# Eight input loads of the first batch asked for by GpSimd's queue instead of SyncE's, in an RWKV and Fourier-mixing kernel on one core

## The chip, the core and the metric

The kernel runs on one core of a Trainium2 chip. The metric is device time in microseconds (us). Before the change the median of three runs is 185.66 us (185.46 to 186.11). One execution was taken by the hardware profiler: it took 186.69 us, of which 184.6 us are the span that the profile shows. Times below that name a place ("at 8.86") are us from the start of that span.

## What is computed

Inputs r, k, v, w have the shape 4 batches x 8 heads x 768 steps x 48, in float32. The first half is a recurrent attention:

```python
for t in range(S):
    cur = einsum('bhd,bhe->bhde', u * k[t], v[t])
    y[t] = einsum('bhd,bhde->bhe', r[t], state + cur)
    state = w[t][..., None] * state + einsum('bhd,bhe->bhde', k[t], v[t])
```

The result, seen as 768 rows of 384 per batch, goes through a mixing block: the real part of a Fourier transform over both axes is added to it, each row is brought to mean 0 and variance 1, and a two-layer network follows (384 to 1536, relu, 1536 to 384), whose result is added to the rows:

```python
u = x + real(fft(fft(x, axis=1), axis=2))
un = (u - mean(u)) / sqrt(var(u) + 1e-6)
out = u + relu(un @ w_ch1) @ w_ch2
```

## The kernel before

**Tiling.** Each batch is cut into 6 chunks of 128 steps; `attention(b, c)` does one. It needs four loads, one each of w, k, r and v, of 128 x 384 float32 (192 KB). In HBM a head's step is a run of 48 floats, so one load moves 1024 pieces of 192 bytes. Here a load is called by tensor, batch and chunk: r(0,1) is r of batch 0, chunk 1. Seven buffers per tensor hold loads that are ahead of the work.

What a chunk does, in lines of the profile: ScalarE takes the logarithm of w (tile `lb`, L533) and casts v to bf16 (`vb`, L533); TensorE adds the logarithms up by triangular matrices (L724, L728, L734, L737); ScalarE takes exponentials (L730, L743, tile `e`); VectorE and GpSimd form the products `rk` (r times k, then times u, L519), `dc` (their sum over a head, L751), `vtd` (v times that sum, L519) and the scaled `rkh` (L519 for k, L762 for r); TensorE transposes these (L778, L784; evictions `rkt`, L542 or L543) and makes the scores (L794), VectorE masks them (L799, `ah`), TensorE multiplies by v and by the state (L820, L841, L844), and VectorE adds `vtd` (L850).

`mix(b)` then does the Fourier sums (L908, L931), the statistics (L933 to L939), the normalised rows `un` (L524 or L533), their transposes (L954, evicted to `unt`) and the two layers (L978 with the first weight matrix, called W1, and L996 with the second, W2). W1 and W2 are asked for once, by GpSimd's queue (L702), and become bf16 on their way; `W_AFTER` makes W1's ask wait for w(0,3) and W2's for r(1,0).

**Order.** Nothing is scheduled at run time. Every piece of work is recorded as an operation, and the table `ORDER` says, engine by engine, in which order the operations stand; "sp" is SyncE's list, which holds the loads (`load_one`, L563), the stores and a few transposes by DMA, and "pool" is GpSimd's. Each engine runs its list strictly in order, and an operation waits by semaphores for those it depends on. `_Prog.schedule` replays the list with fixed costs; the only things taken from its times are the PSUM bank of each tile and the order in which an instruction's waits are written. 32 matmuls that compute nothing (L1053, "warm") stand in TensorE's list to fill gaps, and 26 more stand at its beginning (L1017).

In the opening SyncE asks for r(0,0), k(0,1), w(0,1), u, k(0,0), v(0,0), w(0,0), w(0,2), r(0,1), k(0,2), r(0,2), r(0,3), w(0,4) and so on; GpSimd's list begins with ten fills and index patterns, and its next work is the scaled k of chunk 2 (L519, `rkh`).

Of the kernel before, what the change touches and what calls it, by code (L numbers as in the profile page):

```python
# [7 lines left out]
ALU = mybir.AluOpType  # L8
# [19 lines left out]

W_AFTER = {"W1": (0, 3, "w"), "W2": (1, 0, "r")}

NW = 32
# [4 lines left out]
        "6 74 1438 1439 1440 1441 1442 101 100 127 103 153 129 155 70 113 126 1443 1444 165 112 119 139 138 116 "  # L36
        "66 142 1445 1446 1447 1448 205 179 181 178 152 121 207 1449 1450 68 1451 1452 1453 1454 145 164 147 190 "
        "191 171 1455 168 1456 1457 231 217 194 255 204 1458 173 1459 1460 242 230 216 197 1461 1462 1463 1464 "
        "1465 220 1466 241 263 256 1467 427 199 426 257 1468 245 429 225 264 223 455 265 485 456 1469 248 458 "
        "258 266 259 487 271 272 273 274 275 468 260 276 267 277 278 268 279 280 281 282 303 294 439 438 445 304 "  # L40
        "285 305 286 287 467 295 296 323 332 314 333 324 315 474 325 471 334 310 292 301 316 497 359 343 345 349 "
        "347 355 442 353 351 339 484 365 361 330 477 321 363 357 382 367 368 372 496 448 373 500 369 513 503 514 "
        "516 386 374 506 547 525 388 526 548 384 398 529 390 532 550 377 580 535 581 559 378 560 396 591 379 566 "
        "592 563 394 406 777 779 595 776 568 404 400 392 402 598 806 808 407 613 789 788 411 805 412 408 621 622 "
        "792 614 615 623 616 624 617 625 618 605 626 606 627 607 608 609 610 628 629 630 631 632 864 835 837 866 "
        "653 795 635 636 654 655 644 645 646 637 416 818 817 413 417 673 824 821 664 665 666 660 418 651 674 642 "
        "675 853 834 847 798 705 715 703 707 701 699 898 827 693 900 846 863 711 682 697 695 876 683 713 850 684 "
        "717 722 882 897 931 910 718 709 856 875 909 671 723 879 913 719 680 727 885 724 1117 930 1119 728 689 "
        "729 916 750 918 942 941 742 1116 732 1143 1145 752 746 736 1132 945 734 1169 748 1142 1171 744 738 955 "
        "948 754 740 971 766 972 1129 767 973 1158 1168 956 768 957 958 974 963 975 959 960 1155 976 977 978 979 "  # L50
        "980 981 982 964 965 966 967 968 1135 985 1184 999 1000 1001 986 987 1195 1023 1197 1194 1009 992 1226 "
        "1256 993 1024 1025 994 761 762 763 1016 1181 1228 1161 1017 1018 1010 1011 1225 756 757 1210 1207 758 "
        "1187 1255 1055 1045 1039 1035 1051 1033 1037 1049 1041 1047 1043 1213 1057 1067 1238 1062 1058 1053 "
        "1068 1243 1082 1080 1059 1076 1084 1241 1267 1063 1069 1072 1092 1285 1270 1277 1286 1088 1287 1278 "
        "1064 1279 1074 1293 1294 1295 1094 1296 1297 1280 1281 1298 1282 1299 1300 1288 1301 1302 1303 1304 "
        "1289 1290 1086 1307 1321 1308 1314 1331 1309 1322 1323 1090 1078 1315 1345 1316 1338 1339 1096 1332 "
        "1101 1346 1333 1347 1340 1106 1102 1097 1107 1098 1103 1108 1365 1355 1357 1361 1367 1369 1377 1371 "
        "1363 1359 1394 1414 1373 1402 1406 1398 1412 1416 1379 1404 1375 1384 1400 1396 1380 1389 1408 1381 "
        "1390 1423 1385 1391 1386 1410 1428 1424 1418 1419 1425 1420 1429 1430 1433 1434 1435"),
    "act": (  # L60
        "0 20 21 22 23 24 25 26 109 99 125 151 102 104 156 130 128 71 115 61 140 141 177 203 167 67 182 154 180 "
        "161 135 208 166 69 229 193 233 219 206 187 238 244 232 218 62 454 425 213 243 483 430 459 252 428 457 "
        "435 261 269 283 284 441 270 488 447 440 469 309 291 311 293 344 346 338 360 348 499 356 350 340 354 312 "
        "366 322 486 358 383 313 493 364 512 341 476 515 517 546 387 505 549 527 528 385 522 389 579 551 391 582 "
        "556 561 583 399 534 562 397 593 775 594 395 780 342 588 778 862 804 393 401 403 541 809 405 790 807 574 "
        "791 604 785 833 619 611 633 838 814 843 620 867 797 634 820 819 659 650 641 662 826 652 643 849 836 716 "
        "706 896 708 702 872 663 704 700 1115 901 865 906 696 698 714 855 929 878 933 899 670 712 710 911 691 "
        "672 679 688 692 681 938 1125 884 932 690 1167 1141 891 1120 751 944 943 1118 1177 1146 753 747 737 733 "
        "735 1151 1144 749 1224 739 745 741 1134 755 954 924 1172 1170 1254 1160 961 1193 983 969 970 984 1198 "
        "1196 1005 1258 991 998 1229 1186 1227 1203 1056 1046 1040 1036 1007 1008 1038 1022 1052 1015 1257 1042 "  # L70
        "1050 1044 1263 1212 1031 1032 1081 1083 1219 1249 1073 1077 1089 1276 1093 1075 1095 1305 1291 1085 "
        "1079 1292 1087 1313 1327 1320 1337 1374 1370 1395 1353 1403 1364 1407 1405 1329 1376 1397 1417 1413 "
        "1401 1330 1409 1354 1411"),
    "dve": (
        "30 43 32 45 50 47 33 49 37 53 7 64 31 52 46 8 5 41 10 9 27 35 11 15 12 13 14 17 16 38 18 36 28 29 19 63 "
        "59 34 56 58 55 60 57 105 75 106 39 131 111 110 107 137 65 136 114 157 133 118 117 144 120 159 184 122 "
        "143 162 188 146 185 148 215 192 172 170 169 196 214 195 174 198 239 211 221 222 236 200 247 246 226 224 "
        "228 202 249 464 250 466 251 460 437 436 470 465 462 446 306 288 297 307 298 308 289 299 290 335 300 336 "
        "302 326 337 472 317 473 327 318 319 444 443 328 329 320 331 362 433 478 352 494 475 498 491 502 501 504 "
        "523 370 449 507 557 375 520 531 530 554 533 536 589 538 590 584 537 567 565 564 586 597 569 596 380 786 "  # L80
        "599 571 600 573 601 572 602 603 794 781 793 409 815 783 796 656 647 657 638 648 658 639 649 825 640 823 "
        "661 414 667 676 812 822 419 844 799 870 668 828 669 694 848 677 904 873 854 841 678 852 685 686 687 851 "
        "912 907 857 877 883 880 881 720 914 886 915 1123 887 939 725 730 917 936 919 1126 1149 921 947 946 743 "
        "1152 1133 949 951 950 923 1131 1130 1159 1178 769 1156 1157 1136 1185 1002 988 1003 989 1004 1204 995 "
        "990 996 997 1026 1175 1183 1182 1012 1027 1235 1019 1209 764 1162 1028 1201 1013 759 1020 1021 1188 "
        "1208 1014 1029 1034 1232 1048 1214 1211 1264 1239 1234 1240 1054 1244 1261 1246 1060 1242 1217 1268 "
        "1269 1070 1271 1273 1272 1274 1065 1275 1283 1284 1306 1310 1324 1311 1325 1312 1317 1326 1318 1319 "
        "1334 1348 1091 1349 1341 1342 1335 1336 1350 1343 1351 1344 1109 1358 1362 1368 1099 1356 1378 1366 "
        "1372 1104 1360 1399 1382 1387 1415 1392 1426 1421 1431 1436"),
    "pool": (  # L90
        "42 54 48 4 1 44 40 2 51 3 163 132 108 158 183 189 134 160 209 124 123 210 240 186 234 149 235 175 212 "
        "150 237 176 201 227 253 254 461 463 262 431 495 432 489 490 434 492 518 524 519 552 553 521 558 555 585 "
        "540 539 787 587 570 782 810 816 612 811 784 839 845 868 840 874 869 813 902 903 908 1121 842 1122 934 "
        "905 935 1147 940 871 1148 888 1124 890 1127 937 920 889 1153 922 952 1179 953 1199 962 1173 1150 1205 "
        "1174 1200 1230 1259 1265 1231 1176 1236 1202 1233 1216 1215 1218 1260 1262 1245 1248 1247"),
    "sp": (
        "77 80 79 73 76 78 72 83 81 84 85 89 91 87 88 86 92 82 93 98 94 90 95 450 96 421 479 97 424 453 451 422 "
        "480 423 452 481 482 508 510 509 542 543 544 511 575 545 577 576 772 771 578 800 858 773 832 371 829 774 "
        "803 802 801 381 831 860 830 376 859 894 893 892 925 1113 861 1111 1112 895 926 1139 927 410 1163 415 "
        "1138 420 928 1166 1114 1137 1191 1250 1140 1220 1190 1251 1189 731 1165 1128 1164 1154 1192 1252 1223 "  # L100
        "1221 1222 1180 726 1206 1006 721 1237 760 1253 765 1030 1266 770 1066 1071 1328 1061 1352 1100 1105 "
# [985 lines left out]
```

## Time and profile before

| what | value |
|---|---|
| median of 3 runs | 185.66 us (185.46 to 186.11) |
| profiled execution, its span | 186.69 us, 184.6 us |
| TensorE busy in the span | 175.4 us (95%) |
| VectorE, ScalarE, GpSimd busy | 154.4, 126.6, 103.6 us |
| SyncE's DMA queue (q1) | 26.36 MB, 69.8% of 16 DMA engines' span |
| GpSimd's DMA queue (q0) | 2.36 MB, 7.7% |
| one load of 192 KB, ask to landing | median 3.9 to 4.0 us |
| W1 and W2, ask to landing | 10.5 and 16.2 us |

"Busy" is the time in which an engine executes; asks for transfers are not counted as busy. The rows "SPq" are SyncE's asks. [...] The chain of waits follows the execution back from its end, at each step to what released the step.

### The profile page before, as it was taken

To read this page: it belongs to the slowest core of one execution; us is meant where nothing else is said; L and a number is where in the kernel's file an instruction comes from. 1 tells how busy PE (TensorE), PEld (TensorE's weight loads), DVE (VectorE), ACT (ScalarE), POOL (GpSimd) and SP (SyncE) were. 2 spreads that over 40 slices of the span, in tenths; PEclk is the share of its full clock that TensorE was granted. 3 is DMA by queue.
4 is the path that set the end of the run, shared out by engine and by line. 5 is a ranking of instruction groups with operands and counts; after the bars stand their busy time and mean duration, and the time that the engine had idled before them with its cause. 6 is when DMAs were issued, how large, how long until landed. Compare 5 with 4: busy or idle time off the path is not lost.

```text
span 184.6 us, 4537 instructions
## 1 busy us (share of the span) xinstructions
PE 175.4 (95%) x1718; PEld 114.0 (62%) x1718; DVE 154.4 (84%) x360; ACT 126.6 (69%) x297; POOL 103.6 (56%) x125
## 2 busy tenths in 40 slices
PE   4988997988999999999999999999999999999994
PEld 2555654665566667767667766766666765665663
DVE  8779997999978999999998979999988878771134
ACT  4879696486885999798989897973852653125410
POOL 4038997775416967199899994999287100000000
DMA  6999998999999989999999997974780024330033
GB/s 122 205 203 196 183 208 159 196 187 187 184 190 188 201 168 242 204 219 209 186 250 185 212 216 117 220 140 107 170 181 0 4 85 97 74 109 22 0 128 128
DMA packets 116486, 28.99 MB, mean 157 GB/s; under 512 B 111345, under 2 KB 116082, under 8 KB 116466
## 3 DMA queue, kind: packets, MB, share of 16 engines
q1 hardware_dynamic: 114514, 26.36, 69.8%
q0 software_dynamic: 1952, 2.36, 7.7%
q8 instruction: 13, 0.21, 0.5%
q14 instruction: 7, 0.06, 0.1%
HBM read 23.59 MB, written 4.72 MB: 153 GB/s over the span
## 4 chain that ended last, share of the span: by engine, by line
PE 80%; POOL 7%; DVE 6%; DMA 2%; SPq 2%; issue 1%; ACT 1%; POOLq 0%; DVEq 0%; ACTq 0%
PE bank L996 26%; PE bank L978 26%; PE bank L931 6%; PE bank L908 3%; PE bank L1017 3%; PE bank L794 3%; DMA in_r<-in_r_dram 2%; SPq L563 2%; POOL rk L519 2%; PE bank L844 2%; PE bank L724 2%; PE bank L841 1%; PE bank L728 1%; POOL vtd L519 1%; PE bank L820 1%
## 5 line engine op out<-in xcount | busy, mean ns | idle before, releaser
L996 PE MATMUL bank<-w,ht 128*128 128x384 bf16 (+2 forms) x300 | 53.7, 320 | 0.0
L978 PE MATMUL bank<-unt,w 128*128 128x384 bf16 x288 | 53.3, 326 | 0.2 <-DVE unt L543 0.2
L985 ACT ACTIVATE ht<-bank 128x384 bf16<-128x384 f32 x78 | 35.6, 494 | 25.3 <-PE bank L978 25.0
L996 PEld LDWEIGHTS bank<-w,ht 128*128 128x128 bf16 x300 | 27.5, 98 | 15.8 <-issue 0.2
L978 PEld LDWEIGHTS bank<-unt,w 128*128 128x128 bf16 x288 | 26.8, 97 | 16.3 <-ACT unt L542 0.3
L799 DVE TENSOR_TENSOR ah<-bank,msk 128x512 bf16<-128x512 f32 x48 | 31.4, 680 | 3.3 <-PE bank L794 3.1
L519 POOL TENSOR_TENSOR vtd<-in_v,dc 128x384 f32<-128x384 f32 x24 | 20.7, 863 | 12.1 <-DVE dc L751 10.8
L519 POOL TENSOR_TENSOR rk<-rk,ub 128x384 f32<-128x384 f32 x22 | 22.9, 1042 | 6.9 <-DVE rk L519 6.7
L519 POOL TENSOR_TENSOR rkh<-in_k,e 128x384 bf16<-128x384 f32 x18 | 18.2, 1008 | 12.1 <-ACT e L743 12.0
L1000 DVE SCALAR_TENSOR_TENSOR osb<-bank,rstd,uf 128x384 f32<-128x384 f32 (+2 forms) x25 | 14.8, 594 | 11.8 <-PE bank L996 11.5
L519 POOL TENSOR_TENSOR rk<-in_r,in_k 128x384 f32<-128x384 f32 x18 | 18.0, 1000 | 4.3 <-DMA in_r<-in_r_dram 4.3
L542 ACT ACTIVATE rkt<-bank 128x512 bf16<-128x512 bf16 x29 | 16.9, 603 | 0.5 <-PE bank L778 0.2
L743 ACT ACTIVATE e<-bank 128x392 f32<-128x392 f32 (+1 forms) x24 | 11.7, 496 | 5.3 <-PE bank L737 3.0
L850 DVE TENSOR_TENSOR x<-bank,vtd 128x384 f32<-128x384 f32 x24 | 13.1, 551 | 2.3 <-PE bank L844 2.3
L730 ACT ACTIVATE bank<-bank 128x384 f32<-128x384 f32 x24 | 11.4, 479 | 4.4 <-PE bank L724 4.3
L533 ACT ACTIVATE un<-uf,agg 128x384 bf16<-128x384 f32 x18 | 10.6, 615 | 4.7 <-DVE agg L939 4.5
L933 DVE TENSOR_TENSOR uf<-bank,x 128x384 f32<-128x384 f32 x24 | 12.5, 546 | 1.4 <-PE bank L931 1.3
L762 DVE TENSOR_TENSOR rkh<-bank,in_r 128x384 bf16<-128x384 f32 x24 | 13.1, 548 | 0.7 <-ACT bank L730 0.6
L751 DVE TENSOR_REDUCE dc<-rk 128x8 f32<-128x384 f32 x24 | 12.9, 540 | 0.0
L937 DVE BATCH_NORM_STATS2 bst<-uf 128x6 f32<-128x384 f32 x24 | 12.7, 548 | 0.1
L533 ACT ACTIVATE vb<-in_v 128x384 bf16<-128x384 f32 x22 | 11.2, 520 | 1.8 <-DMA in_v<-in_v_dram 1.7
L533 ACT ACTIVATE lb<-in_w 128x384 bf16<-128x384 f32 x24 | 11.9, 520 | 0.6 <-DMA in_w<-in_w_dram 0.4
(128 smaller groups left out, 332.2 us busy)
## 6 DMA issues: line engine op xcount, KB each, us to landing
in_r<-in_r_dram SPq DMA_DIRECT2D x24, 192.0 KB, 3.9
in_k<-in_k_dram SPq DMA_DIRECT2D x24, 192.0 KB, 3.9
in_w<-in_w_dram SPq DMA_DIRECT2D x24, 192.0 KB, 3.9
in_v<-in_v_dram SPq DMA_DIRECT2D x24, 192.0 KB, 4.0
out_dram<-osb SPq DMA_DIRECT2D x23, 192.0 KB, 2.3
w<-in_moe_w_ch_dram POOLq DMA_DIRECT2D x2, 1152.0 KB, 13.4
out_dram<-osb SPq DMA_DIRECT2D x1, 128.0 KB, 1.8
rkt<-rkh SPq DMA_TRANSPOSE x6, 3.3
```

Of the source, the lines that this page charges most:

```text
L519: return lambda e: e.tensor_tensor(out=o, in0=a, in1=b, op=f)
L533: return lambda e: e.activation(o, a, f, **kw)
L542: {"act": lambda e: e.activation(o(), i(), ACTF.Copy), "dve": lambda e: e.tensor_copy(out=o(), in_=i())}, **kw)
L751: op("dve", v_1(DM), lambda e: e.tensor_reduce(out=dc[:, :], in_=rku[:, :, :], axis=mybir.AxisListType.X, op=ALU.add), r=[("RK", i2)], w=[ ...
L762: op("dve", v_1(DM), lambda e: e.tensor_tensor(out=rh[:, :, 0:D], in0=ps(tce)[:, 0:DM].rearrange("t (h d) -> t h d", d=D), in1=rt[:, :, :] ...
L799: masked[n] = op("dve", v_1(512), lambda e, x=x: e.tensor_tensor(out=ah[:, x:H:2, :], in0=ps(ta[x])[:, :].rearrange("p (h t) -> p h t", t= ...
L850: op("dve", v_1(DM), lambda e: e.tensor_tensor(out=xb[:, c, 0:DM], in0=ps(ty)[:, 0:DM], in1=vtd[:, :, :].rearrange("t h d -> t (h d)"), op ...
L937: op("dve", v_1(DM), lambda e, kb=kb, bs=bs: e.bn_stats(bs[:, :], uf[:, kb, :]), r=[("UF", i, kb)], w=[("BST", n % 4)])
L978: ins = e.matmul(ps(t)[:, 0:384], W1[:, m, 128 * j:128 * j + 128], unt[:, :, m, :], start=(m == 0), stop=(m == NM - 1))
L985: "act": lambda e, j=j, t=t, ht=ht: e.activation(ht[:, j, :], ps(t)[:, 0:384], ACTF.Relu, scale=-1.0)},
L996: ins = e.matmul(ps(t)[:, 0:hi - lo], ht[:, j, 128 * x:128 * x + 128], W2[:, j, lo:hi], start=(j == 0), stop=(j == NJ - 1))
L1000: op("dve", v_1(hi - lo) + 64, lambda e, kb=kb, t=t, o=o, lo=lo, hi=hi: e.scalar_tensor_tensor(out=o[:, lo:hi], in0=ps(t)[:, 0:hi - lo], s ...
```

## The change

Eight of the 24 loads of batch 0 are taken out of SyncE's list and put into GpSimd's, directly after its ten opening fills, in the order v(0,1), k(0,2), v(0,2), w(0,3), r(0,3), v(0,3), r(0,5), v(0,5). They have semaphores of their own and wait for nothing. SyncE's list is otherwise unchanged, and so is the order of all real work on every engine.

```diff
+LOAD_POOL = ((0, 1, 'v'), (0, 2, 'k'), (0, 2, 'v'), (0, 3, 'r'), (0, 3, 'w'), (0, 3, 'v'), (0, 5, 'v'), (0, 5, 'r'))
...
-        o = op("sp", 750, lambda e: e.dma_start(INB[n][i][:, :, :],
+        o = op(*(("pool", 1000) if (b, c, n) in LOAD_POOL else ("sp", 750)), lambda e: e.dma_start(INB[n][i][:, :, :],
                                                 src[n][b, :, c * CH:(c + 1) * CH, :].rearrange("h t d -> t h d")),
-               w=[("in", n, i)], sem="in_%s%d" % (n, i), xfer=960)
+               w=[("in", n, i)], sem=("gin_%s%d" if (b, c, n) in LOAD_POOL else "in_%s%d") % (n, i), xfer=1006)
...
-NW = 32
+NW = 41
...
     "pool": (
-        "42 54 48 4 1 44 40 2 51 3 163 132 108 158 183 189 134 160 209 124 123 210 240 186 234 149 235 175 212 "
...
+        "44 56 50 4 1 46 42 2 53 3 84 86 88 89 91 92 98 100 165 134 110 160 185 191 136 162 211 126 125 212 242 "
...
     "sp": (
-        "77 80 79 73 76 78 72 83 81 84 85 89 91 87 88 86 92 82 93 98 94 90 95 450 96 421 479 97 424 453 451 422 "
...
+        "79 82 81 75 78 80 74 85 83 87 93 90 94 95 96 97 452 423 481 99 426 455 453 424 482 425 454 483 484 510 "
...
+        for x, val in enumerate((1.0 / DM, DM ** -1.5)):
+            op("dve", 40, fill(MUC[:, x:x + 1], val), w=["MUC"])
```

(The numbers in the lists are shifted by 2 because of the two small fills, `MUC`, that VectorE now does in its opening and that nothing reads.)

There are 41 warm matmuls instead of 32, and some stand elsewhere in TensorE's list: 8 instead of 5 ahead of the first L728; single ones moved in the first 36 us; one before the first L931 that reads `hcr`; and seven around the first three transposes of `un` (L954), namely one ahead of the first, two between the first and the second, three between the second and the third, and one just ahead of the first L978.

The replay's costs for transfers changed (`xfer` 960 to 1006 and two lines of `schedule`), and with them the PSUM banks of 794 operations; 19 TensorE operations now wait for other evictions than before. Further code that the diff brings in is switched off by its constants: joint transposes (`JOIN_T = 24`, with 24 chunks numbered 0 to 23), loads of two chunks at once (`LOAD_2 = 4`, with batches 0 to 3), weights in parts (`W_PARTS = (1, 1)`), other statistics (`MEAN_FIRST = 0`) and a split first layer (`SPLIT_FIRST = 0`). The buffers stay at seven per tensor.

## The prediction

> **What bounds the kernel now.** I read the busy time by stretches first. Its columns are the stretch, its length, then busy us of TensorE, of its weight loads, VectorE, ScalarE and GpSimd, the granted clock, the DMA engines' busy share and GB/s.
>
> ```profile
> 5.00:10.00 5.00, 5.00 (x24) 2.48 (x23) 3.42 (x17) 4.55 (x9) 0.00 (x0) 1.00 1.05 205
> 46.00:50.00 4.00, 4.00 (x34) 2.35 (x32) 3.69 (x8) 3.42 (x8) 1.40 (x2) 1.00 1.27 184
> 50.00:172.00 122.00, 122.00 (x1195) 80.82 (x1193) 105.52 (x226) 87.84 (x216) 72.85 (x78) 1.00 0.74 152
> ```
>
> From 46 to 172 TensorE has no idle time at full clock. What the change does up to the first W1 matmul (L978 at 45.41) therefore reaches the end one for one, and nothing later can be gained. GpSimd is idle in 5 to 10, so asks placed there displace no work.
>
> Then the chain of waits, from the opening to that matmul (start, length, what):
>
> ```profile
> 9.59 0.92 PE bank L1053 x5
> 10.50 0.16 PE bank L728
> 10.67 0.18 PE bank L724
> 10.84 0.02 issue
> 10.87 0.47 ACT bank L730
> 11.34 0.41 ACT e L743
> 11.75 0.02 issue
> 11.78 0.56 DVE rkh L519
> ...
> 33.14 4.07 DMA in_r<-in_r_dram
> ```
>
> From 11.78 to 28.99 it runs through VectorE and GpSimd, then through SyncE's asks and the load r(1,1), which lands at 37.21. Loads are also what these engines waited for in 28 to 46 (us in all, times, longest):
>
> ```profile
> ACT vb L533 <- DMA in_v<-in_v_dram: 1.3, 1, 1.3
> POOL vtd L519 <- DMA in_v<-in_v_dram: 1.1, 1, 1.1
> DVE rk L519 <- DMA in_r<-in_r_dram: 0.6, 1, 0.6
> ```
>
> The first two end at 30.48 and 30.60, when v(0,4) lands. So earlier loads can gain something around 30 and 37, and later ones can lose something in the opening.
>
> **How two queues share the DMA engines.** Before the change SyncE's queue (q1) and GpSimd's (q0) run together only while the weights come. Packets in 45 to 50, then in 51.5 to 52.5, where q1 drains what had piled up:
>
> ```profile
> q0 software_dynamic: 961, 0.74, 93.7%
> q1 hardware_dynamic: 963, 0.18, 33.6%
> ```
> ```profile
> DMA packets 1263, 0.25 MB, mean 250 GB/s; under 512 B 1244, under 2 KB 1263, under 8 KB 1263
> ```
>
> With work in both, the queues take turns packet by packet, whatever the sizes (961 to 963). Here both would carry 192-byte packets, so each gets half. The engines can move 250 GB/s of such packets; q1 alone reached 205 in 5 to 10. A load of 192 KB is 0.79 us at 250 GB/s and 0.96 us at 205.
>
> **Step 1, the opening, a loss.** GpSimd's last fill ends at 2.44. W1's ask took 0.93 us and W2's 1.06, so eight asks of about 1 us end at 10.5, ahead of its first work at 12.22. W1, asked for at 34.35, had its first packet at 36.27, so the first of the eight moves from about 4.4. The loads that SyncE's list needs at once are still in its own queue, and w(0,0), w(0,2) and r(0,1) now take turns with v(0,1), which is not needed until 19.6, and others. I let q1 keep its full rate to 5.0. In the trace r(0,1) was asked for at 6.50 and landed 3.8 us later, at 10.28; from 5.0 that is 5.28 us at 0.97 us a load (its queue's landings are so far apart), or 5.4 loads. At half of 250 GB/s a load takes 1.57 us, 5.4 take 8.5, and r(0,1) lands at 13.5. VectorE forms r times k of chunk 1 (0.49 us at 10.84) ahead of the scaled k (11.78 in the chain); it would start at 13.55, and the scaled k at 14.05. w(0,2), which lands at 9.63 now, would land at 12.5 and hold ScalarE's exponentials to about the same point. The chain is late by **D = 2.3 us**.
>
> Inside D lie the three more warm matmuls ahead of the first L728: by the row above (5 in 0.92) they are 0.5 us, which is what D comes to if no load is late. GpSimd's own eight loads land 1.57 us apart from 6.0 to 17.0, ahead of their times in the trace (v(0,1) at 19.6, k(0,2) at 11.5, r(0,5) at 26.3, others between). VectorE's two fills (0.06 each) lie ahead of the logarithms' 0.2 us wait for w(0,0).
>
> **Step 2, later waits that go, a gain.** From 4.4 to 17.0 the engines move 16 loads instead of 13, and SyncE has eight asks less (0.7 to 1.3 us each, 7.2 in all by their rows), so v(0,4) and r(1,1) land earlier while the work is D later. The wait at v(0,4) is worth 1.12 us: TensorE's scores (L794 at 31.55) had been free since 30.43. The wait at r(1,1) frees VectorE 0.56 earlier; but what it leads to is the first L931 on `hcr` at 41.48, for which TensorE had been free since 40.90, and there the changed banks and one more warm matmul cost it 0.31 + 0.16 (L784 and L820 now wait for evictions that ended 0.3 us after these started). So 0.27 of the 0.58 is left, and the gain is **1.4 us**. W1 is asked for D less 1.06 later (GpSimd's part of the same wait), so lands at 44.85 + 1.2; L978 comes later than that. W2 no longer waits 1.3 us for r(1,0), and follows W1 as now.
>
> **Step 3, warm matmuls ahead of L978, a loss.** Three now stand between the second and third transpose of `un`, one just ahead of L978:
>
> ```profile
> 44.21 0.66 PE L954 MATMUL bank<-idw,un 128*128 128x128 bf16 x6 [0.32 <-ACT un L533]
> 45.41 0.81 PE L978 MATMUL bank<-unt,w 128*128 128x384 bf16 x4 [0.15 <-DVE unt L543]
> ```
>
> The second transpose ends at 44.38 and the third starts at 44.53; three of 0.163 end at 44.87, so the third, its eviction and L978 are **0.35 us** later. The other three lie in a gap (43.72 to 44.21) or cover none. If W1 were what L978 waits for, the 0.35 would be hidden.
>
> **Sum.** 2.3 - 1.4 + 0.35 = +1.2 us, rounded. The profiled execution would go from 186.69 to 187.9; it lies 1.0 above the median, so the median goes from 185.66 to **186.9 us**.
>
> Two bounds of D: no load late, 0.5; the two queues together no faster than one, 205 GB/s, which gives 1.92 us a load, r(0,1) at 15.4 and D = 4.2. I take 250 because q1 reached it with a backlog, and two queues have one. Banks beyond those named: in the trace the newly awaited evictions ended before their waiters started, bar up to 0.3 us in L778, L784, L820 and L931 between 38 and 45; I count them in step 2 and nowhere else.
>
> **Rivals.**
>
> *No bandwidth gained.* The two queues only divide the 205 GB/s of 5 to 10. For it: the busy share is over 1 there already (1.05). Against: it is 1.27 in 46 to 50. D = 4.2, the sum +3.1, 188.8 us. [...]
>
> *The urgent loads pass (other side: not slower).* If what SyncE asked for by 6.5 keeps its rate, because GpSimd's transfers start late or slowly, D is the 0.5 us of warm matmuls, the gains stay, and the sum is 0.5 - 1.4 + 0.35 = -0.55: 185.1 us. For it: while W1's first packets came slowly, 15 in 36.3 to 36.9, q1 moved 349. Against: packets then went one to one. The point that decides is r(0,1)'s landing: before 12.3 the sum is below 0. [...]
>
> *GpSimd's asks last longer.* Above 1.22 us each they end after 12.22, and GpSimd's first work is late. At 1.6 us, half as much again as W2's, they end at 15.2, 3.0 late, and what VectorE waits for from GpSimd follows: about +1.9, 187.6 us. Against: 0.93 and 1.06.
>
> **How the numbers follow.** Half shares at about 250 GB/s 0.45, no bandwidth gained (or q0 preferred) 0.20, urgent loads pass 0.25, longer asks 0.10. The first alone spans 186.2 to 187.5 (230 to 280 GB/s). The range takes in the second and third: 185.0 to 188.9. 0.3% is 0.56 us, about what a measurement of this kernel can tell from no change. Faster by more holds a good part of the third case, 0.22; the same takes its rest and the edge of the first, 0.20; slower 0.58.
>
> **What would show it.** Step 1: r(0,1) landing near 13.5 and w(0,2) near 12.5, q0 and q1 packets in equal number in 5 to 15 at about 250 GB/s, the scaled k of chunk 0 near 14; GpSimd's asks ending near 10.5. Step 2: no wait for v(0,4) or r(1,1), the first L931 on `hcr` about 0.9 later than 41.48. Step 3: warm matmuls ahead of the third transpose while its input is ready. L978 near 46.6 and unbroken work after. It is wrong if the scaled k starts before 13, or if TensorE idles after 46.6.

## The result and the profile after

The changed kernel takes **193.49 us** (median of 4 runs, 193.11 to 193.65), the kernel before on the same chip 185.88 (185.46 to 186.20): a ratio of 1.041, interval 1.038 to 1.044. Slower was forecast, but by 1.2 us and not by 7.6; the time lies outside the range. The profiled execution took 193.34 us, its span is 190.5 (before: 186.69 and 184.6). All ratios here and below are between executions in the faster of two states in which the kernels are met; two profiled executions, of the second kernel of experiment 1 (196.91) and of the casting loads in experiment 3 (197.68), fell in the slower one, so nothing rests on the trace of the first, and less on that of the second. Lines of the code have moved: L563 is now L590, L728 L766, L519 L538, L524 L543, L543 L562, L931 L976, L937 L1002, L954 L1019, L978 L1045, L1053 L1121.

Busy time by stretches of the kernel after, with the columns of the first table of the prediction:

```profile
5.00:10.00 5.00, 5.00 (x27) 2.58 (x26) 3.98 (x18) 3.44 (x6) 5.00 (x6) 1.00 1.21 241
10.00:15.00 5.00, 1.68 (x13) 0.61 (x11) 0.56 (x2) 0.94 (x2) 0.04 (x1) 1.00 1.09 212
15.00:20.00 5.00, 2.92 (x26) 1.90 (x27) 2.55 (x7) 2.74 (x7) 1.54 (x2) 0.58 1.24 207
20.00:25.00 5.00, 5.00 (x63) 3.67 (x62) 4.89 (x9) 4.38 (x10) 3.48 (x4) 0.74 1.01 196
```

From 10 to 15 TensorE is busy a third of the time and the other engines stand nearly still, while the DMA engines work all the time (busy share 1.09): something is being loaded, but not what is needed. Behind it TensorE's granted clock falls to 0.58 and 0.74; in the trace of before it is 1.00 in every stretch. The chain of waits says what everybody waited for (start, length, what):

```profile
7.04 0.04 issue
7.08 10.24 DMA in_r<-in_r_dram
17.32 0.03 issue
...
17.42 0.56 DVE rk L538
17.98 0.48 DVE rkh L538
```

SyncE asks for r(0,1) at 7.08, and it lands 10.24 us later, at 17.32; before, it landed at 10.28, 3.8 us after its ask, and the prediction had it at 13.5. Who had the DMA engines meanwhile, in 12 to 14 (queue: packets, MB, share of the 16 engines' time):

```profile
q0 software_dynamic: 139, 0.42, 98.4%
q1 hardware_dynamic: 140, 0.03, 11.5%
```

The packets of the two queues are equal in number, 139 to 140. But one of GpSimd's carries on average some 16 times the bytes of one of SyncE's (419 KB in all against 27): the packets of the eight loads are of 4224 and 3840 bytes (22 and 20 runs of 192 bytes merged; 102 of the 139, the other 37 are of 4 bytes), SyncE's are of one run. The kernel before had shown the same. This is its own trace, in 38 to 44, while W1 came, a stretch that the prediction did not look at:

```profile
q0 software_dynamic: 468, 1.07, 94.6%
q1 hardware_dynamic: 447, 0.09, 13.0%
```

Nearly one to one in packets, 92 to 8 in bytes: 315 of the 468 are W1's, of 3072 bytes each (one row of 1536 bf16 numbers), and 138 are W2's, of 768. The stretch that the prediction did use, 45 to 50, holds W2's alone, and there too the bytes were 0.74 to 0.18 MB.

Following every instruction from before to after gives the sum as it was. VectorE's scaled k of chunk 0 starts at 17.89 instead of 11.78, **6.11 late**. By 22.4 this has grown to 6.9, in two steps: 0.36 at VectorE's eviction at 20.64, which waits for transposes that TensorE does at a granted clock of 0.50 (the last four take 0.63 us, the same four 0.39 before), and 0.41 in VectorE's next product r times k, which takes 0.95 us beside a product of GpSimd's (20.70 to 21.52) where it took 0.55 before:

```profile
20.98 0.95 DVE L538 TENSOR_TENSOR rk<-in_r,in_k 128x384 f32<-128x384 f32 x1
```

At v(0,4) 1.36 us come back, at the first L976 on `hcr` 0.32 more (5.23 late there, at 46.70). The first L1045 is 5.90 late, and nothing changes after it. In 7 to 15 the queues moved 216 GB/s together. The last steps ahead of that L1045 in TensorE's list:

```profile
49.76 0.33 PE L1019 MATMUL bank<-idw,un 128*128 128x128 bf16 x3
49.93 0.65 PE L1121 MATMUL bank<-idw,msk 128*128 128x384 bf16 x3
50.43 0.33 PE L1019 MATMUL bank<-idw,un 128*128 128x128 bf16 x3
51.30 0.48 PE L1045 MATMUL bank<-unt,w 128*128 128x384 bf16 x2
```

### The profile page after: what moved, and what is told of

Same layout as the page of the kernel before. It is cut to its first block, busy times and chain, and to the rows that moved or that the text cites. A ratio compares the mean times of both kernels' runs of the same rounds, so it can differ in the third digit from the quotient of the medians.

```text
span 190.5 us, 4558 instructions
## 1 busy us (share of the span) xinstructions
PE 178.9 (94%) x1727; PEld 116.1 (61%) x1727; DVE 156.0 (82%) x362; ACT 126.4 (66%) x297; POOL 110.6 (58%) x133
## 4 chain that ended last, share of the span: by engine, by line
PE 78%; DVE 7%; DMA 5%; ACT 3%; SPq 3%; issue 1%; POOL 1%; DVEq 0%
PE bank L1064 25%; PE bank L1045 25%; DMA in_r<-in_r_dram 5%; PE bank L976 5%; PE bank L953 4%; PE bank L839 3%; SPq L590 3%; PE bank L824 2%; PE bank L889 2%; PE bank L819 2%; PE bank L762 2%; DVE ah L844 2%; ACT rkt L561 2%; PE bank L886 2%; PE bank L766 1%; PE bank L1019 1%
## 5 line engine op out<-in xcount | busy, mean ns | idle before, releaser
L1045 PE MATMUL bank<-unt,w 128*128 128x384 bf16 x288 | 53.3, 326 | 0.0
L1053 ACT ACTIVATE ht<-bank 128x384 bf16<-128x384 f32 x78 | 35.6, 494 | 26.1 <-PE bank L1045 25.9
L1064 PEld LDWEIGHTS bank<-w,ht 128*128 128x128 bf16 x300 | 27.5, 98 | 15.8 <-issue 0.2
L1045 PEld LDWEIGHTS bank<-unt,w 128*128 128x128 bf16 x288 | 26.8, 97 | 16.2 <-issue 0.2
L538 POOL TENSOR_TENSOR vtd<-in_v,dc 128x384 f32<-128x384 f32 x24 | 20.3, 847 | 16.2 <-DVE dc L789 16.1
L538 POOL TENSOR_TENSOR rk<-rk,ub 128x384 f32<-128x384 f32 x22 | 22.8, 1038 | 8.1 <-DVE rk L538 7.8
L538 POOL TENSOR_TENSOR rkh<-in_k,e 128x384 bf16<-128x384 f32 x18 | 18.2, 1010 | 11.2 <-ACT e L781 11.2
L538 POOL TENSOR_TENSOR rk<-in_r,in_k 128x384 f32<-128x384 f32 x18 | 18.0, 1001 | 0.0
L1002 DVE BATCH_NORM_STATS2 bst<-uf 128x6 f32<-128x384 f32 x24 | 12.8, 549 | 0.1
L766 PE MATMUL bank<-lb,nle 128*128 128x384 bf16 x24 | 7.4, 334 | 5.3 <-ACT lb L552 5.3
```

The lines of the kernel that those rows point to most:

```text
L538: return lambda e: e.tensor_tensor(out=o, in0=a, in1=b, op=f)
L1002: op("dve", v_1(DM), lambda e, kb=kb, bs=bs: e.bn_stats(bs[:, :], uf[:, kb, :]), r=[("UF", i, kb)], w=[("BST", n % 4)])
L1045: ins = e.matmul(ps(t)[:, 128 * x0:128 * (x0 + nx)], W1[:, m, 128 * j:128 * j + 128], unt[:, x0:x0 + nx, m, :], start=(m == 0), stop=(m == ...
L1053: "act": lambda e, j=j, t=t, ht=ht: e.activation(ht[:, j, :], ps(t)[:, 0:384], ACTF.Relu, scale=-1.0)},
L1064: ins = e.matmul(ps(t)[:, 0:hi - lo], ht[:, j, 128 * x:128 * x + 128], W2[:, j, lo:hi], start=(j == 0), stop=(j == NJ - 1))
```

## The experiments

Kernels built on the one before get a helper behind the replay that takes an operation out of one engine's list and puts it into another's, so PSUM banks and warm matmuls stay as they were. Each kernel was compared with runs of the kernel before on its own chip, and the ratio is to those. "Landed" and "at" are us from the span's start.

**1. The loads alone, and the rest alone.**

```diff
+    for x, key in enumerate(((0, 1, "v"), (0, 2, "k"), (0, 2, "v"), (0, 3, "w"), (0, 3, "r"), (0, 3, "v"), (0, 5, "r"), (0, 5, "v"))):
+        move(loads[key], "pool", 10 + x)
```

> The kernel before with one part of the change alone: the same eight loads are asked for by GpSimd in the same order; warm matmuls, PSUM banks and fills stay as before. Theory A (GpSimd's queue sends packets of about 22 runs of 192 bytes, SyncE's packets of one run, the queues take turns by packet, and so SyncE's urgent loads stand still until GpSimd's are through): r(0,1) lands at 17 to 17.5 as it did after the change, the chain is 6 us late, the later gain of 1.7 stays, and with 0.6 to 0.8 for a slower TensorE clock the median is 5.5 to 7.0 above before. Rival B (half shares, as predicted, and the rest of the loss comes from banks and warm matmuls): r(0,1) near 13.5, median 0.9 to 1.5 above before.

Measured: 193.42 us (193.17 to 193.58), ratio 1.031 (1.025 to 1.036); r(0,1) landed at 17.55, VectorE's first work on it 6.8 late, the span is 191.2. That is close to the landing of theory A and within its time, and far from rival B's.

The other way round, the kernel after with the eight loads back in SyncE's list:

> The kernel after with its eight loads back in SyncE's list at their places of before: warm matmuls, banks and fills alone. Theory A: the loads do it all, and what is left is the 0.67 us that the trace shows ahead of the first W1 matmul, plus up to 0.5 for three warm matmuls more ahead of the first logarithm sums: 0.4 to 1.1 above before. Rival B: 5 us or more above before, with r(0,1) landing where it did before (10.3 to 10.5).

Measured: ratio 1.000 (0.995 to 1.004), that is 0.9 us below to 0.7 above before, where 0.4 to 1.1 above had been expected. The loads make the loss. Warm matmuls, banks and fills make none of it that this interval can show.

**2. Another second queue.** The same loads asked for by ScalarE's queue:

```diff
+        move(loads[key], "act", 1 + x)
```

> The kernel before with the same eight loads asked for by ScalarE's queue, right after its first table load. Theory A (it is the size of GpSimd's packets): ScalarE's transfers go in packets of one run like SyncE's, the turns are fair, and r(0,1) lands between 13.5 (both queues together at 250 GB/s) and 15.4 (at 205). ScalarE's own work starts about 6 us later for its eight asks, which it has some 3 us of idle time for, so the time is 2 to 4.5 above before. Rival C (whichever queue is asked in bulk first is served first, packets or not): r(0,1) at 17 or later and the time 6 or more above before.

Measured: 194.17 us, ratio 1.035 (1.031 to 1.039); r(0,1) landed at 16.46. The shares were even (from 7 to 15 0.90 MB for SyncE's queue, 0.84 for ScalarE's, landings 1.80 us apart in each). The landing lies between the two theories, and for a reason that I had not reckoned with: ScalarE's queue sent its first packet at 2.45, GpSimd's at 5.07, so that much more was put ahead of r(0,1). That left the sizes of the two causes open, and the first ask was held back until a VectorE fill had ended:

```diff
+        move(loads[key], "act", 1 + x)
+        loads[key].deps.add(g.ops[35])
```

> The kernel before with the eight loads asked for by ScalarE's queue, the first ask waiting for a VectorE fill that ends at 3.3, so that the queue's first packets come at about 5.1, as GpSimd's did after the change (5.07), instead of 2.45. Packets of one run on both sides, equal shares, 1130 runs per us together as in the first run with ScalarE. If equal shares had been the case after the change, r(0,1) would land where it lands here: worked out from 1.8 us per load and 4.7 to 5.4 loads ahead of it at 5.1, between 13.6 and 15.0. What is missing to the 17.3 to 17.9 beside GpSimd's queue is the price of its larger share; what is above 13.5 that of 217 GB/s instead of 250. If r(0,1) lands at 16.5 or later, shares made no difference. ScalarE's own work waits behind its asks, so the time says nothing.

Measured: r(0,1) landed at **14.53** (in the one execution that there is; the time, 196.64, says nothing, as said). The queues of this kernel in 7 to 15 (q10 is ScalarE's, q1 SyncE's), and below them those of the kernel after in the same stretch:

```profile
q10 hardware_dynamic: 4961, 0.94, 72.5%
q1 hardware_dynamic: 4563, 0.86, 65.6%
```
```profile
q0 software_dynamic: 438, 1.33, 77.5%
q1 hardware_dynamic: 2062, 0.39, 35.5%
```

ScalarE's packets are of one run like SyncE's, and SyncE's queue keeps 48% of the bytes; beside GpSimd's it keeps 23%. But the even share does not come from turns packet by packet. In 10 to 11 of this kernel, and below it in 11 to 13, first one queue and then the other has most of the packets:

```profile
q10 hardware_dynamic: 1016, 0.19, 123.6%
q1 hardware_dynamic: 129, 0.02, 15.9%
```
```profile
q1 hardware_dynamic: 1817, 0.34, 111.2%
q10 hardware_dynamic: 489, 0.09, 29.4%
```

SyncE's and ScalarE's queues are ahead in turn by 900 to 1300 packets here, about a load of 1024. So this kernel gives the price of equal shares, however they come about, and does not test the packet's size; experiment 3 does. Of the way from 13.5 (predicted) to 17.32 (measured), 1.0 us is what equal shares would have cost beyond my reckoning, and 2.8 us is GpSimd's larger share (up to 3.3 by the landings at 17.55 in experiment 1 and at 17.80 in a second profile of the kernel after).

**3. Packets of another size in GpSimd's queue.** Eight extra loads that nothing reads, all loads of the kernel before left with SyncE; once in float32, once cast to bf16 on the way:

```diff
...
+        o = op("pool", 1000, lambda e, to=to, x=x: e.dma_start(
+            to, src["v"][3, :, CH * (x % 6):CH * (x % 6) + CH, :].rearrange("h t d -> t h d")), w=[("extra", x)], sem="extra", xfer=960)
...
+        g.order["pool"].insert(10 + x, o)
...
```

> The kernel before, all loads asked for by SyncE as before, and eight extra loads by GpSimd at the time of the change's eight: 128 x 384 float32 of batch 3, in runs of 192 bytes, into the memory of W1 and W2, whose own asks wait for them. Nothing reads them. Theory A (large merged packets of GpSimd's queue starve SyncE's): packets of about 4 KB in GpSimd's queue, SyncE's queue nearly still while they run, r(0,1) at 17 to 17.5. No load is taken off SyncE's list, so all its later loads are late by eight loads as well (7 to 8 us): 7 to 9.5 above before. Rival B (half shares): r(0,1) near 14.

Measured: 194.68 us, ratio 1.045 (1.038 to 1.052), r(0,1) at 18.81: later than any theory said, with SyncE's queue at 20% of the bytes in 7 to 15.

> As the extra loads in float32, but the eight become bf16 on their way, as W1 and W2 do, whose packets in the trace of before were one run each. Same asks, same runs read, same times. Theory A (it is the packet's size): packets of one run, the two queues' packet counts alternate one to one, and from the first packet of GpSimd's queue (about 5.6) the 4.7 loads that SyncE still has ahead take 1.8 us each, as they did beside ScalarE's queue (1.80 us from landing to landing): r(0,1) lands at 13.5 to 15, at least 2 us earlier than beside the float32 ones. In the end SyncE's loads still wait for the extra bytes: 5 to 9 above before, so the landing decides, not the time. Rival C (GpSimd's queue is served first whatever its packets): r(0,1) at 17 again.

Measured: 195.93 us, ratio 1.049 (1.040 to 1.058). The casting packets are of one run (96 bytes written), and in 7 to 15:

```profile
q0 software_dynamic: 5642, 0.53, 124.5%
q1 hardware_dynamic: 3307, 0.62, 64.1%
```

SyncE's queue gets 37% of the runs instead of 20%, so the packet's size matters (or the cast, which changed along with it). But the packets are not one to one, as they had been beside W2 (961 to 963): 63% of them are GpSimd's. r(0,1) landed at 16.97, 1.8 earlier than beside the float32 loads, but where rival C had it and 2 us later than theory A. So A is not the whole of it, and why GpSimd's queue keeps more than half even with small packets stays open.

**4. Fewer loads, early or late.** Only r(0,5) and v(0,5) go to GpSimd, first at the head of its list, then with their asks held until r(0,1) has landed:

```diff
+    for x, key in enumerate(((0, 5, "r"), (0, 5, "v"))):
+        move(loads[key], "pool", 10 + x)
+        loads[key].deps.add(loads[0, 1, "r"])
```

> The kernel before with only r(0,5) and v(0,5) asked for by GpSimd at the head of its list. If the loss in the opening is the volume put ahead of r(0,1) at 205 to 217 GB/s, two loads make r(0,1) 1.8 to 1.9 later (12.1 to 12.3), and VectorE's first work on it 1.3 to 1.5. The waits for v(0,4) and r(1,1) then give 1.1 to 1.4 back, as the bytes ahead of them are the same: 0 to 0.6 above before. If a second queue at this point disturbs SyncE's beyond its bytes, r(0,1) is later than 12.5 and the time over 1 above.

Measured: 187.27 us, ratio 1.004 (1.000 to 1.007); r(0,1) landed at 12.19, VectorE's first work on it 1.45 late; 0.21 late after v(0,4), 0.39 **early** at r(1,1), and 0.51 late at 44.5. As forecast, up to the last step: 0.9 us are lost between 39.4 and 44.5, and the warm matmuls are those of before. Half of it is in one instruction. VectorE in this kernel, then GpSimd beside it, then VectorE in the kernel before:

```profile
44.11 0.87 DVE L524 TENSOR_SCALAR un<-uf,agg 128x384 bf16<-128x384 f32 x1
```
```profile
43.77 0.99 POOL L519 TENSOR_TENSOR rk<-in_r,in_k 128x384 f32<-128x384 f32 x1
44.84 1.00 POOL L519 TENSOR_TENSOR rk<-rk,ub 128x384 f32<-128x384 f32 x1
```
```profile
44.06 0.41 DVE L524 TENSOR_SCALAR un<-uf,agg 128x384 bf16<-128x384 f32 x1
```

What put GpSimd there is an earlier load. Before the change GpSimd stood idle at this point for 4.31 us, waiting for r(1,2), which landed only at 48.5, behind the weights:

```profile
48.52 1.00 POOL L519 TENSOR_TENSOR rk<-in_r,in_k 128x384 f32<-128x384 f32 x1 [4.31 <-DMA in_r<-in_r_dram]
```

With two loads less on its list SyncE asks for r(1,2) early enough that it lands ahead of the weights (at 36.9), GpSimd starts at once, and the two engines meet. VectorE's instruction takes 0.87 us beside GpSimd against 0.41 alone: it starts at 44.11 and ends at 44.98, 0.22 us after GpSimd's first product (44.76). Why it takes longer there is not shown.

> The same two loads, but GpSimd's asks wait until r(0,1) has landed. The opening loses nothing (first VectorE work on r(0,1) within 0.2 of before). But the loads of SyncE's list land just in time from 15 to 26.5 (w(0,3) 0.24 ahead of its use, k(0,3) 0.37, r(0,4) 0.44, k(0,5) without slack), and two loads passed ahead of them make them 1.5 to 1.9 late: by this theory the time is 0 to 0.8 above before, and no place in the first 26 us is free. Rival: once the urgent ones are through there is room, and the time is 0.5 to 1.4 below before, by the waits for v(0,4) and r(1,1) alone.

Measured: 189.11 us, ratio 1.014 (1.006 to 1.023), above what either side said. The opening loses nothing (r(0,1) at 10.2), the just-in-time loads cost 1.9 to 2.9 by 21 (TensorE's clock is 0.50 from 16.4 to 19.8), the waits give back 1.3 and 0.6, the meeting costs 0.5 (0.88 us again), and then 1.7 come at 46 to 50, where the granted clock falls to 0.50 during the first W1 matmuls. That last part neither theory had.

**5. The clock.** Warm matmuls in TensorE's idle time of the kernel after, first 18 and 12:

> The kernel after with 18 more warm matmuls ahead of the first logarithm sums and 12 ahead of the second, in stretches in which TensorE stood idle (10.6 to 13.8 and 14.8 to 17.0). If the granted clock of about 0.5 in 16 to 22.5 is a result of that idle time and costs the chain what I read from the trace (0.6 to 0.8 us), the clock is 1.0 from 10 on and the time 0.5 to 0.9 below after. If the slow clock costs nothing, because TensorE is not what ends the waits there, the time is within 0.3 of after. If the clock drops whatever TensorE does, the row shows it again.

Measured: 196.38 us, ratio 1.046 (1.041 to 1.052). The trial failed by its own making. The clock dropped at 15.5 all the same, and the 12 matmuls stood between two loads: at a granted clock of 0.50 they and one that stood there already took 4.3 us (17.44 to 21.76) on the path. So all 30 were put ahead of the first logarithm sums:

```diff
+    first = [o for o in pe if o.idx == 103][0]
+    for x in range(30):
+        o = op("pe", mm(384), warm, r=["MSK", "IDB"], w=[tw])
...
+        pe.insert(pe.index(first), o)
```

> The kernel after with 30 more warm matmuls, all of them ahead of the first logarithm sums, so that TensorE is busy from 9 to about 15.5 and none of them stands between the loads w(0,2) and r(0,1) and what they release. If the granted clock of 0.5 from 16 to 22.3 comes from TensorE's idle time in 10.6 to 17, the clock now stays at 1.0 and the time is 0.5 to 0.9 below after. In the first trial with more warm matmuls TensorE had been busy up to 13.4 and the clock dropped at 15.8 all the same; if it drops again at about that time, idle time just before it is not the cause, and the time is within 0.3 of after.

and beside it the kernel after unchanged:

> The kernel after unchanged, as the reference for the two runs beside it: 7.0 to 8.0 above before, r(0,1) landing at 17 to 17.6.

Measured: 192.89 us (192.27 to 193.57) against 194.12 (192.78 to 194.44). The granted clock now stays at 1.00; the stretches of the kernel with 30 more:

```profile
15.00:20.00 5.00, 3.26 (x36) 1.67 (x35) 2.17 (x5) 3.85 (x10) 1.09 (x2) 1.00 0.88 167
20.00:25.00 5.00, 4.74 (x68) 3.20 (x68) 5.00 (x12) 4.73 (x12) 4.25 (x4) 1.00 0.91 177
```

The medians differ by 1.2, but the ratios to the kernel before, 1.032 (1.028 to 1.037) and 1.037 (1.032 to 1.043), overlap, and the unchanged kernel's openings vary too: r(0,1) landed at 17.32 and 17.80 in its two profiles. So the price is read from the traces. Against the first profile of the kernel after, VectorE's scaled k starts 0.49 later here (w(0,0) landed at 16.13 instead of 13.12) and its work at 22 is 0.32 earlier (0.37 at the first L1045), a gain of 0.81 by 22. Of this 0.35 come up to the eviction that had waited for TensorE's transposes, now at 20.78. The other 0.4 is the product that GpSimd had held up:

```profile
21.11 0.55 DVE L538 TENSOR_TENSOR rk<-in_r,in_k 128x384 f32<-128x384 f32 x1
```

So the clock of 0.50 costs 0.4 us by itself, and 0.8 if that meeting is counted as its consequence, which was not tried apart. The slow stretches here last 6.8, 6.8 and 3.4 us (after, the failed trial, each of the two in the kernel with two late loads). In the failed trial TensorE had been busy to 13.4, 2.1 us ahead of the drop at 15.5; in the kernel with 30 more it was busy throughout 10 to 15, and the clock stayed at 1.00. How much idle time brings the clock down is not shown.

**6. The meeting of VectorE and GpSimd.** The kernel after, with GpSimd's product held until VectorE's is through:

```diff
+    g.ops[491].deps.add(g.ops[302])
```

> The kernel after with one wait more: GpSimd's r times k of chunk (1,2), L538, waits for VectorE's third normalised rows un (L543), which took 0.88 us beside it instead of 0.41 before the change. Before the change GpSimd stood idle there, as r(1,2) landed only at 48.5. If this meeting of the two engines is what most of the step of 0.67 us ahead of the first W1 matmul is, the instruction takes 0.41 again, and the time is 0.3 to 0.5 below after. If the warm matmuls moved there are the step, as I had predicted (0.35), the instruction may be short again, but the time stays within 0.15 of after.

Measured: 193.56 us (192.98 to 194.06) against 194.12. The instruction takes 0.41 again:

```profile
49.37 0.41 DVE L543 TENSOR_SCALAR un<-uf,agg 128x384 bf16<-128x384 f32 x1
49.70 0.55 DVE L1002 BATCH_NORM_STATS2 bst<-uf 128x6 f32<-128x384 f32 x1
50.75 0.36 DVE L562 COPY unt<-bank 128x384 bf16<-128x384 bf16 x1 [0.50 <-PE bank L1019]
```

but VectorE then waits 0.50 us for TensorE, whose third transpose stands behind the three warm matmuls and starts at 50.38 (50.43 in the kernel after). Of the 0.51 won, 0.05 are left at the last eviction ahead of the first L1045, which itself starts at 51.42 (51.30 after). So the warm matmuls alone hold this place as much as the meeting alone does where there are none of them (experiment 4), and taking the meeting away wins nothing. The medians' 0.56 comes from openings that differ.

**7. What the rest of the sum is worth, and a better order.** SyncE alone asks for all, three of the eight loads between the urgent ones, so that r(0,1) lands where equal shares were predicted to put it:

```diff
+    for key, nxt in (((0, 1, "v"), (0, 0, "w")), ((0, 2, "k"), (0, 2, "w")), ((0, 2, "v"), (0, 1, "r"))):
+        move(loads[key], "sp", g.order["sp"].index(loads[nxt]))
```

> The kernel before with one queue and another order in it: SyncE asks for v(0,1), k(0,2) and v(0,2) ahead of w(0,0), w(0,2) and r(0,1), one by one in turn. r(0,1) then lands three loads of 0.95 later, at 13.1, which is nearly where I had predicted it for equal shares (13.5). If the rest of the sum holds, VectorE's first work on it is 2.3 late, 1.1 to 1.4 comes back at v(0,4) and r(1,1), up to 0.5 is lost to the meeting with GpSimd, and the time is 0.9 to 1.9 above before, with up to 0.8 more if the granted clock drops after TensorE's idle time. If the time is 3 or more above, a late r(0,1) costs more than the sum says, whatever made it late.

Measured: ratio 1.010 (1.004 to 1.015), some 1.9 us; r(0,1) landed at 13.37, VectorE's first work on it 2.63 late, 2.90 at the first W1 matmuls. The forecast's upper end: the waits do give 1.2 and 0.6 back, but other parts of the opening (4.1 late by 22, with TensorE's clock at 0.50 from 15.3 to 18.7) and the meeting (0.87 us again) take more than I had given them.

Last, two versions that keep one queue and ask for v(0,4) and r(1,1) earlier, to have the gain without the loss:

> The kernel before, all loads in SyncE's queue; only two of them stand earlier in its list: v(0,4) directly ahead of w(1,2), one place, and r(1,1) directly ahead of k(1,0), three places. If the later gain that the change showed (1.36 us at v(0,4), 0.32 at the first L931 on hcr) comes from when these two loads land and from nothing else in the second queue, it comes without the opening's loss: the chain to the first W1 matmul is 1.0 to 1.5 us earlier, and the time 0.8 to 1.4 below before. Rival: what is won at these waits is lost again before the first W1 matmul, as in the run with two early loads (0.9 us between 39.9 and 44.5, half of it one VectorE instruction L524 that took 0.87 us instead of 0.41 while GpSimd worked beside it): then 0 to 0.5 below.

Measured: ratio 1.005 (1.001 to 1.010), slightly slower. v(0,4), asked for 0.8 earlier, landed at 30.40 instead of 30.46: in both traces a 16 KB instruction transfer of 0.93 us starts at 28.0 to 28.2, with v(0,4) in flight (that this is why it lands late was not tried). And r(1,0), now one place later, held up W2's ask and with it GpSimd, 2.84 us instead of 1.31; the 0.71 won at r(1,1) became 0.74 lost.

> The kernel before with k(1,2) asked for two places later by SyncE, behind r(1,1), so that r(1,0) and r(1,1) land 0.7 to 1.0 earlier; k(1,2), used at 42.26, would land at 37.4. No load moves ahead of another that is just in time, W2's ask by GpSimd (waiting for r(1,0)) comes earlier and not later, and r(1,2) still lands behind the weights. The first L931 on hcr gains 0.3 to 0.58 (TensorE is free 0.58 earlier), and the time is 0.2 to 0.6 below before. Rival: the gain is lost at a meeting of GpSimd and VectorE ahead of the first W1 matmul, as in three runs before: the time is within 0.2 of before.

Measured: ratio 1.000 (0.995 to 1.006). The first L931 on `hcr` did come 1.14 earlier, and then the first W1 matmul waited for W1 itself:

```profile
PE bank L978 <- DMA w<-in_moe_w_ch_dram: 1.0, 1, 1.0
POOL rk L519 <- DMA in_r<-in_r_dram: 0.9, 1, 0.9
```

Before the change W1 landed at 44.85, 0.56 ahead of that matmul, so no more than about 0.6 can be won ahead of it unless W1 lands earlier. Asking for it earlier was not enough: here it was asked for at 33.90 instead of 34.35 and landed at 45.47. In this execution TensorE's clock then fell to 0.50 from 45.5 to 48.9, and its span, 186.4, is longer than most of its kernel. No version here beats the kernel before.

## Why the prediction was wrong

**The step that failed is step 1**, the opening's D = 2.3, in the words "Here both would carry 192-byte packets, so each gets half". The first half of its ground, "the queues take turns packet by packet", held in number after the change (139 to 140 packets in 12 to 14). The packets were not alike (4224 and 3840 bytes against 192). D was 6.1, and r(0,1) landed at 17.32. With equal shares (experiment 2, second kernel) r(0,1) landed at 14.53 instead of 13.5: the 1.0 is for "The engines can move 250 GB/s". That kernel's two queues moved 225 GB/s in 7 to 15 (216 after the change), and the prediction's 5.4 loads at half of 225 take 9.4 us instead of 8.5. The other 2.8 is the larger share of GpSimd's queue, 77% of the bytes. The size of the packets is a part of it by experiment 3 (r(0,1) 1.8 earlier with small ones, if it was not the cast); beyond it GpSimd's queue has 63% of the packets there, which is not explained. A stretch of the trace of before (38 to 44) stood against the assumption; I had read only the one with W2.

**A cost that no step had:** 0.8 us by 22.4, of which 0.4 is TensorE's clock, which fell to 0.50 at 15.8, after the idle time that the late load made, and 0.4 is VectorE's product beside GpSimd. Experiment 5, in which the clock stays up, has neither; that the second follows from the first is not shown. Here a loss in waiting cost more than the waiting.

**Step 2 was right** in its places and near in size: 1.4 predicted, 1.36 + 0.32 = 1.68 measured, at the two places named. Its working has a slip: 0.58 less 0.31 and 0.16 leaves 0.11, not 0.27, so the sum by its own terms is 1.4 and not 1.2. What it left out is that earlier loads also start GpSimd earlier (experiments 4 and 6).

**Step 3 was right in what it named, and incomplete**: 0.35 predicted, 0.67 measured. The warm matmuls hold the third transpose as described: the second is 5.55 late, the third 5.90. The other 0.32 lies between the first L976 on `hcr` and the second transpose, and was not followed further. VectorE's slower instruction stands beside the warm matmuls and would cost 0.5 without them. The three more warm matmuls ahead of the first L728 cost nothing that shows (experiment 1, second kernel).

**The rivals.** "No bandwidth gained" came nearest in time (188.8) and was nearer on the bandwidth (216 GB/s measured, against 205 and 250), but took equal shares for granted; its working put r(0,1) at 15.4. "Urgent loads pass" is refuted (its point of decision was 12.3; measured 17.32). "Asks last longer" is refuted: the eight asks took 1.42 and then 0.89 to 0.95 us and ended at 10.04. The place in which the truth lay, a share below half for SyncE's queue, was mentioned in a bracket ("or q0 preferred") and never priced.

The sum as measured on the trace: 6.1 for D, some 0.8 by 22.4, less 1.7, plus 0.67, is 5.9 in the span; the profiled execution's time outside the span was 0.75 longer than before (2.84 against 2.09), and the execution profiled before the change lay 0.8 above its median.

## What to carry to other kernels

Before moving transfers to another queue, look at the size of a packet in each of the two queues. Between SyncE's and GpSimd's queues here the packets came in equal number in 12 to 14 (139 to 140), and the queue with the small ones was left with 6% of the bytes there and 23% in 7 to 15; its urgent loads nearly stood still (r(0,1) took 10.24 us instead of 3.8). Then measure the shares, for the same two queues did not always go one to one (5642 packets to 3307 beside the casting loads). Here, where loads land just in time, eight others put ahead of them cost nearly their whole volume (r(0,1) landed 7.0 late; eight loads at 0.96 are 7.7): the two queues moved 216 GB/s in 7 to 15, one alone 203. That GpSimd was idle in 5 to 10 did not make the DMA engines idle (busy share 1.05). And a load that lands earlier is not only a wait less: ask which engine it sets going, and beside what (0.87 us instead of 0.41 for VectorE beside GpSimd).

## What the runs showed of the hardware that was not expected

- GpSimd's queue put 22 or 20 runs of 192 bytes into a packet in the eight loads of the change (256 packets of 4224 bytes, 128 of 3840), and one run into each packet of the casting loads (5642 packets for 0.53 MB in 7 to 15). SyncE's and ScalarE's queues sent one run in a packet (4563 for 0.86 MB and 4961 for 0.94 MB in the second kernel of experiment 2).
- Two queues together hardly moved more than one with such runs: 214 to 225 GB/s in 7 to 15 where SyncE's list has eight loads less, 199 beside the eight extra float32 loads, 203 before with one queue.
- SyncE's and ScalarE's queues, both with packets of one run, did not go one to one in the second kernel of experiment 2: 1016 packets of ScalarE's to 129 of SyncE's in one microsecond, 489 to 1817 in the next two.
- TensorE's granted clock fell from 1.00 to 0.50 after stretches in which TensorE was idle or only partly busy, for 3.4 us (the kernel with two late loads), 6.8 (after) or 10.2 (the first kernel of experiment 2 and both of experiment 3). After the change the matmuls from 15.8 to 22.6, around the late landing of r(0,1) at 17.32, were slow in this way.
- One VectorE instruction of 0.41 us took 0.87 beside GpSimd, and a product of two inputs 1.20 instead of 0.49 (VectorE's first work on r(0,1) in the first kernel of experiment 7, where GpSimd's scaled k ran from 13.27 to 14.26).
